# Blocks of 256 rows throughout, expert weights in two transfers, and more low halves on VectorE, in a convolution with eight experts

## The chip, the cores and the metric

One core of one Trainium2 chip. The metric is device time in microseconds (us) of one execution. Three runs of the kernel before gave 1292.79, 1296.68 and 1301.12 us; their median is 1296.68 us.

## What is computed

A softmax-weighted causal convolution over 28672 rows of 192 values is followed by a layer of eight experts, of which each row uses the one with the largest gate product:

```
w   = softmax(weight_gen, over the 7 taps)                 # per row and head
x   = sum over taps k of w[.., k] * x_pad[row + k]         # (28672, 192)
e   = argmax(x @ w_gate)                                   # 8 experts
h   = max(x @ w1[e], 0)                                    # 192 -> 1024
out = prob[e] * (h @ w2[e])                                # 1024 -> 192
```

## The kernel before, in words

The convolution runs in 16 chunks (**stages**) of 14 x 128 = 1792 rows. It is VectorE's main work: lines 358 (products) and 363 (sums), in fp32. Behind a chunk's last sum, line 384 (`halves`) writes the lower fp16 half of its rows, TensorE transposes them (line 398, 42 transposes a chunk) and multiplies them with the gate (line 406, 42 products), VectorE finds the expert and the place of each row (lines 418 to 481, ending in `pos`), and GpSimd scatters the rows, sorted by expert, to a scratch in memory (line 456, 14 scatters a chunk). A table (line 493 on) then says which **blocks** of rows of one expert are complete.

Every number is held as two fp16 halves, so a product is several matmuls. A block's **load** (`load`, from line 549) is four transfers on SyncE's queue: the expert's weights (line 558, 1536.5 KB) and a further 64 partitions of them (line 559, 128 KB), the block's rows `xb`, transposed on the way (line 562), and places and gate factors (line 568). There are three weight buffers, `wt0` to `wt2`. A block then runs in steps of 512 columns of a PSUM bank: with 256 rows four steps, each of 2 x 128 hidden columns; with 512 rows eight steps of 128. In a step the **first products** (lines 594 to 598) fill `p1`, ScalarE takes the upper half of the activated result (`hh`, line 601), and the **low half** `hl` = max(p1, 0) - hh is made in one of two ways: by VectorE in one instruction (line 611), or by TensorE and ScalarE, with a product of `hh` with minus the identity added into `p1` (line 608) and a second activation (line 609). The **second products** (line 627) of `hh` and `hl` follow two to four steps later. `NZ[s]` says how many of the eight slots of a block of stage s go to VectorE; a block of 256 rows uses the first four slots only, so that a 3 there means one of its four. After the last chunk's routing all go to VectorE (`state["done"]`).

The order on each engine is written out ahead of time: `produce()` (the convolution) and `consume()` (the blocks) are two lists of steps with planned times, and the one that is due earlier is written next; TensorE, VectorE, ScalarE and SyncE keep that order. `ahead(n + 1, 2)` in `consume()` issues loads until two blocks beyond the running one are asked for. The last five blocks stand behind conditions; how many of them run depends on the data, here one. All experts' rows together need 115 blocks of 256 rows; the kernel before runs 81 blocks of 256 and 17 of 512.

Of the kernel before, what the change touches and what calls it, by code (L numbers as in the profile page):

```python
# [18 lines left out]
E, F = 8, 1024  # L19
# [6 lines left out]
CAP = N + 256  # L26
TRASH = E * CAP
RW = 400
N256 = 10
SIZES = [(256,)] * N256 + [(512,)] * (len(WID) - N256)  # L30
LAST = 256
PRIO = 2500
# [3 lines left out]
WW = 7 * F + 2  # L36
# [14 lines left out]
LAG2, LAG0, LAGN, LAGL = 2, 4, 1, 4  # L51
HHB, HLB, YB = 6, 6, 12
AV = 4.0
NZ = [0] * 4 + [3] * 12
FINE = 8
DH = 0.65
NSK = 5
# [22 lines left out]
def conv_moe_kernel(ctx: ExitStack, tc: tile.TileContext, x, wgen, wg_in, w1, w2, out):  # L80
    nc = tc.nc
    V, A, GP, PE, SP = nc.vector, nc.scalar, nc.gpsimd, nc.tensor, nc.sync
# [11 lines left out]
    wsc = dram.tile([E, P, WW], F16, name="wsc")  # L94
# [5 lines left out]
    def raw(i):  # L100
        return getattr(i, "ins", i)
# [346 lines left out]
    def no_dep(i, *groups):  # L448
        for g in groups:
            tc.declare_no_dep(i, group=g, reason="rows are disjoint")  # L450
# [87 lines left out]
    nout = [0]  # L538
    loaded = []
    loaded2 = []  # L540
    wts = []
    pools = []

    def written(i, s):

        info = mybir.DependencyInfo(mybir.DependencyClass.Sync, mybir.DependencyReason.DATA)
        for k in scats[s] + (zeros if s == nchunk - 1 else []):
            tc.add_manual_dep(i, k.name, info, reason="rows of the stage")

    def load(s, tb, g, bs):  # L550
        nj = bs // P
        ffn = pools[0]
        with tc.issue_after(loaded[-1]) if loaded else ExitStack():
            rv = SP.value_load(tb[0:1, 0, g:g + 1], min_val=0, max_val=TRASH + 256 - bs)
            ev = SP.value_load(tb[0:1, 1, g:g + 1], min_val=0, max_val=E - 1)
        wt = wts[len(loaded2) % len(wts)]
        loaded2.append(None)
        SP.dma_start(out=wt[:, F:WW], in_=wsc[bass.ds(ev, 1), :, F:WW].rearrange("o p c -> p (o c)"))
        SP.dma_start(out=wt[0:64, 0:F], in_=wsc[bass.ds(ev, 1), 0:64, 0:F].rearrange("o p c -> p (o c)"))
        xb = ffn.tile([P, 3 * 512], F16, name="xb", bufs=3)  # L560
        xv = xb[:, 0:3 * bs].rearrange("p (a b) -> p a b", a=3)
        i = raw(SP.dma_start_transpose(out=xv, in_=scr[bass.ds(rv, bs), 0:384]))
        later = [f"scat{k}" for k in range(s + 1, nchunk)] + ([] if s == nchunk - 1 else ["zero"])
        no_dep(i, *later)
        written(i, s)
        tc.add_to_no_dep_group("loads", i)
        mt = ffn.tile([P, 4, 2], I32, name="mt", bufs=8)
        i = raw(SP.dma_start(out=mt[:, 0:nj, :], in_=scri[bass.ds(rv, bs), 192:194].rearrange("(j p) c -> p j c", p=P)))
        no_dep(i, *later)
        written(i, s)  # L570
        tc.add_to_no_dep_group("loads", i)
        loaded.append(i)
        return wt, xv, mt

    class Block:
        def __init__(self, tiles, bs, via):
# [68 lines left out]
    def step(b=None, f=None):  # L645

        if b is not None:
            b.first(f)
            line.append((b, f))
        n = len(line)  # L650

        def lows(force):
            while at_low[0] < n and (force or n - 1 - at_low[0] >= LAGN):
                g, k = line[at_low[0]]
                g.low(k)
                at_low[0] += 1

        if b is None:
            lows(True)
        more = True  # L660
        while more:
            more = False
            for part, lag in ((1, LAGL), (0, LAG2)):
                i = at_second[part]

                if i < (at_second[0] if part else n) and (b is None or n - 1 - i >= (LAG0 if part == 0 and line[i][1] == 0 else lag)):
                    g, k = line[i]
                    g.second(k, part)
                    at_second[part] += 1
                    more = True  # L670
        if b is not None:
            lows(False)
# [114 lines left out]
    def consume():  # L787
        t = 0.0
        todo = [(s, i, b, bs) for s, stl in enumerate(stages) for i, (bs, g, _) in enumerate(stl) for b in range(g)]
        ready = []  # L790
        skip = todo[len(todo) - NSK:] if NSK else []
        i = raw(SP.dma_start(out=scri[TRASH:TRASH + 256, :].rearrange("(p j) c -> p j c", j=2), in_=zrow.bitcast(I32)))
        no_dep(i, *(f"scat{k}" for k in scats))
        todo = todo[:len(todo) - NSK]

        def ahead(n, k):
            while len(ready) < k and n + len(ready) < len(todo):
                s, i, b, bs = todo[n + len(ready)]
                if s not in avail or (ready and t < avail[s]):
                    break  # L800
                ready.append(load(s, seg_tabs[s][i], b, bs))

        for n, (s, i, b, bs) in enumerate(todo):
            while s not in avail:
                yield None
            if t < avail[s]:
                t = avail[s]
                state["pe"] = 0.0
            yield t
            ahead(n, 1)  # L810
            own = NZ[s] if not state["done"] else NF
            via = [int((k + 1) * own // NF == k * own // NF) for k in range(NF)]
            blk = Block(ready.pop(0), bs, via)
            for k in range(blk.steps):
                with tc.high_priority(offset=PRIO):
                    step(blk, k)
                if k == LAGL - 1:
                    ahead(n + 1, 2)
                if k == blk.steps // 2:
                    blk.gates()  # L820
                t += BLK / NF + NEG * via[k] + state["pe"]
                state["pe"] = 0.0
                yield t
        step()

        def rest(i):
            if i < len(skip):
                loaded.clear()
                with tc.If(cnt > skip[i][2]):
                    for s, j, b, bs in skip[i:i + NSS]:  # L830
                        blk = Block(load(s, seg_tabs[s][j], b, bs), bs, (0,) * NF)
                        for k in range(blk.steps):
                            step(blk, k)
                        blk.gates()
                        step()
                    rest(i + NSS)

        if NSK:
            cnt = nc.values_load(nreal[0][0:1, 0:1], min_val=0, max_val=64)
            rest(0)  # L840
        yield 1e9

    ET = mybir.EngineType
    with tc.manual_schedule(engines={ET.DVE, ET.Activation, ET.PE, ET.SP}):
        pg, cg = produce(), consume()
        tp, tcon = 0.0, None
        with tc.tile_pool(name="stg", bufs=WB) as pool:
            stg.append(pool)
            while not state["prep"]:
                tp = next(pg)  # L850
        pools.append(ctx.enter_context(tc.tile_pool(name="ffn", bufs=2)))
        for i in range(3):
            wts.append(pools[0].tile([P, WW], F16, name=f"wt{i}", bufs=1))
            A.activation(out=wts[i][64:P, 0:F], in_=ones[64:P, 0:1].to_broadcast([64, F]), func=AF.Copy, scale=0.0)
        while tp < 1e9 or tcon is None or tcon < 1e9:
            if tp < 1e9 and (tcon is None or tp + state["own"] <= tcon):
                tp = next(pg)
                if tcon is None:
                    tcon = next(cg)
            else:  # L860
                tcon = next(cg)
# [26 lines left out]
```

## Time and profile before

| | us |
|---|---|
| median of 3 runs | 1296.68 |
| the profiled execution | 1297.31 |
| its span, from first to last instruction | 1295.6 |

In the rows further down, times count from the span's start. A busy TensorE (PE) is not a TensorE at its peak, since the durations of its matmuls overlap; how far apart their starts lie tells its pace. PEld is its weight load. "Idle before" is the time an engine did nothing ahead of an instruction, and the name behind the arrow is what ended it.

### The profile page before, as it was taken

Reading aid. Unit: us, or ns where it says so; the run is one execution under the profiler, and the core shown is the slowest. Engines: PE = TensorE matmul, PEld = TensorE weight load, DVE = VectorE, ACT = ScalarE, POOL = GpSimd, SP = SyncE. Lnnn points to the kernel's source line nnn. Section 1 sums busy time; section 2 is a strip of 40 time slices with the busy share of each in tenths; the row PEclk is TensorE's granted clock in tenths of the full one; section 3 lists DMA queues with packets and bytes.
Section 4 is the critical chain, followed back from the end, with each engine's and each line's share of the span. In section 5 each row is a group of like instructions: output and inputs, shape, how many; then the busy total and the mean of one; then the engine's idle time right before and its main releaser. Section 6 shows DMA issues by size and latency. Waiting matters only on the chain.

```text
span 1295.6 us, 29303 instructions
## 1 busy us (share of the span) xinstructions
PE 1155.5 (89%) x11223; PEld 955.5 (74%) x11223; DVE 998.1 (77%) x1285; ACT 766.1 (59%) x1401; POOL 778.2 (60%) x611
## 2 busy tenths in 40 slices
PE   1485499899999999989998998999999999999997
PEld 0143277788888888888987887776777777789886
DVE  8998999899998999999999999999443333323322
ACT  5888665667775676666766666665743333333332
POOL 3236616558888888988878898888762222222222
PEclk9787799999999999999999999999999999999999
DMA  9747777788879899998889889855777665498883
GB/s 323 229 159 254 240 239 225 233 249 264 269 216 279 221 287 252 275 286 231 281 263 273 245 262 294 231 156 139 192 227 158 145 148 148 138 254 217 239 244 94
DMA packets 190754, 293.94 MB, mean 227 GB/s; under 512 B 135695, under 2 KB 155264, under 8 KB 176017
## 3 DMA queue, kind: packets, MB, share of 16 engines
q1 hardware_dynamic: 168816, 247.02, 66.3%
q0 software_dynamic: 21792, 44.99, 12.2%
q8 instruction: 90, 1.47, 0.5%
q14 instruction: 56, 0.45, 0.1%
HBM read 208.89 MB, written 61.03 MB: 208 GB/s over the span
## 4 chain that ended last, share of the span: by engine, by line
PE 41%; DMA 15%; DVE 15%; POOL 9%; issue 5%; ACT 2%; SPq 1%; POOLq 0%; DVEq 0%; ACTq 0%
PE po L627 18%; DMA xb<-scr 9%; POOL scr L456 7%; DVE tmp L358 5%; DVE acc L363 5%; PE p L594 4%; DMA scr<-rows,pos 4%; PE p L598 4%; PE p L596 4%; PE p L597 4%; PE p L595 4%; DMA out_dram<-y,mt 2%; POOL out_dram L635 2%; PE p L608 2%; DVE rows L384 1%
## 5 line engine op out<-in xcount | busy, mean ns | idle before, releaser
L635 POOL DMA_INDIRECT out_dram<-y,mt x230 | 307.3, 1336 | 340.8 <-ACT y L634 281.7
L601 ACT ACTIVATE hh<-p 128x512 f16<-128x512 f32 x460 | 276.0, 600 | 316.9 <-PE p L598 312.0
L456 POOL DMA_INDIRECT scr<-rows,pos x224 | 387.2, 1729 | 113.8 <-issue 60.4
L627 PE MATMUL po<-wt,hh 128*128 128x192 f16 x3680 | 367.1, 248 | 0.7 <-ACT y L634 0.7
L611 DVE SCALAR_TENSOR_TENSOR hl<-p,hh 128x512 f16<-128x512 f32 x215 | 148.1, 689 | 248.5 <-ACT hh L601 248.5
L627 PEld LDWEIGHTS <-hh 128*128 128x128 f16 x3680 | 314.0, 99 | 7.6 <-issue 0.8
L358 DVE TENSOR_TENSOR tmp<-xin,wgt 128x1344 f32<-128x1344 f32 (+1 forms) x168 | 289.6, 1750 | 1.3
L363 DVE TENSOR_TENSOR acc<-acc,tmp 128x1344 f32<-128x1344 f32 (+1 forms) x168 | 289.4, 1750 | 1.0
L594 PE MATMUL p<-xb,wt 128*128 128x256 f16 (+1 forms) x784 | 228.8, 292 | 51.3 <-DMA xb<-scr 42.8
L609 ACT ACTIVATE hl<-p 128x512 f16<-128x512 f32 x245 | 146.6, 598 | 147.5 <-PE p L608 142.7
L596 PE MATMUL p<-xb,wt 128*128 128x256 f16 (+1 forms) x784 | 229.2, 292 | 0.0
L598 PE MATMUL p<-xb,wt 128*128 128x256 f16 (+1 forms) x784 | 229.2, 292 | 0.0
L597 PE MATMUL p<-xb,wt 128*128 128x256 f16 (+1 forms) x784 | 229.2, 292 | 0.0
L595 PE MATMUL p<-xb,wt 128*128 128x256 f16 (+1 forms) x784 | 229.0, 292 | 0.0
L627 PE MATMUL po<-wt,hl 128*128 128x192 f16 x1840 | 228.1, 247 | 0.0
L627 PEld LDWEIGHTS <-hl 128*128 128x128 f16 x1840 | 165.1, 98 | 33.3
L594 PEld LDWEIGHTS <-wt 128*128 128x128 f16 x784 | 76.7, 98 | 63.9 <-issue 58.1
L595 PEld LDWEIGHTS <-wt 128*128 128x128 f16 x784 | 76.7, 98 | 29.2 <-issue 6.6
L608 PE MATMUL p<-hh,negi 128*128 128x512 f16 x245 | 92.8, 379 | 5.4 <-ACT hh L601 5.4
L598 PEld LDWEIGHTS <-wt 128*128 128x128 f16 x784 | 77.0, 98 | 23.9
L597 PEld LDWEIGHTS <-wt 128*128 128x128 f16 x784 | 77.0, 98 | 23.9
L596 PEld LDWEIGHTS <-wt 128*128 128x128 f16 x784 | 76.9, 98 | 23.9
(123 smaller groups left out, 1100.6 us busy)
## 6 DMA issues: line engine op xcount, KB each, us to landing
wt<-wsc SPq DMA_DIRECT2D x98, 1536.5 KB
xin<-in_x_dram SPq DMA_DIRECT2D x15, 1344.0 KB
wt<-wsc SPq DMA_DIRECT2D x98, 128.0 KB
wgt<-in_weight_gen_dram SPq DMA_DIRECT2D x16, 392.0 KB
wsc<-wt SPq DMA_DIRECT2D x8, 768.5 KB
wa<-in_moe_w_dram SPq DMA_DIRECT2D x8, 768.0 KB
wa<-in_moe_w_dram SPq DMA_DIRECT2D x8, 512.0 KB
wsc<-wt SPq DMA_DIRECT2D x16, 256.0 KB
```

The lines of the kernel that those rows point to most:

```text
L358: V.tensor_tensor(out=t[:, a:b, :].rearrange("p t (h g) -> p (t h) g", g=G), in0=xv, in1=wv, op=ALU.mult)
L363: V.tensor_tensor(out=acc[:, a:b, :], in0=acc[:, a:b, :], in1=t[:, a:b, :], op=ALU.add)
L456: i = raw(GP.indirect_dma_start(scri, bass.IndirectOffsetOnAxis(ap=pos[:, t:t + 1], axis=0), rows_t[s % 3].bitcast(I32)[:, t, 0:RW // 2], ...
L594: PE.matmul(o, lhsT=wt[:, F + fs:F + fs + P], rhs=xv[:, 0, :], start=i == 0, stop=False)
L595: PE.matmul(o, lhsT=wt[:, F + fs:F + fs + P], rhs=xv[:, 1, :], start=False, stop=False)
L596: PE.matmul(o, lhsT=wt[:, 3 * F + fs:3 * F + fs + P], rhs=xv[:, 0, :], start=False, stop=False)
L597: PE.matmul(o, lhsT=wt[:, 2 * F + fs:2 * F + fs + P], rhs=xv[:, 2, :], start=False, stop=False)
L598: PE.matmul(o, lhsT=wt[:, fs:fs + P], rhs=xv[:, 2, :], start=False, stop=i == self.each - 1)
L601: A.activation(out=hh, in_=p1, func=AF.Relu, scale=1.0 - 2.0 ** -11 if self.via[k] else 1.0)
L611: V.scalar_tensor_tensor(out=hl, in0=p1, scalar=0.0, in1=hh, op0=ALU.max, op1=ALU.subtract)
L627: PE.matmul(o, lhsT=h[:, js], rhs=w2, start=(f == 0 and j % 2 == 0 and not part and w == 0), stop=part == 1 and f == NF - 1 and (j % 2 == ...
L635: i = raw(GP.indirect_dma_start(out, bass.IndirectOffsetOnAxis(ap=self.mt[:, j, 1:2], axis=0), y, None, bounds_check=N - 1, oob_is_err=False))
```

## The change

Three things are changed. All 16 stages cut their rows into blocks of 256 (`N256`). The big weight transfer is cut in two: the part for the first products goes out with the 128 KB, x and the places, as before two blocks ahead but already behind a block's first step; the part for the second products goes out by a function of its own, `seconds()`, behind the fourth step, or ahead of the next load. And `NZ` now gives VectorE no low halves up to stage 4 (the stages count from 0), two of a block's four in stage 5 (slots 2 and 4), and all from stage 6.

```
-N256 = 10
+N256 = 16
-NZ = [0] * 4 + [3] * 12
+NZ = [0] * 5 + [5] * 1 + [8] * 10
...
     def load(s, tb, g, bs):
...
+        seconds()
-        SP.dma_start(out=wt[:, F:WW], in_=wsc[bass.ds(ev, 1), :, F:WW].rearrange("o p c -> p (o c)"))
+        SP.dma_start(out=wt[:, F:4 * F], in_=wsc[bass.ds(ev, 1), :, F:4 * F].rearrange("o p c -> p (o c)"))
         SP.dma_start(out=wt[0:64, 0:F], in_=wsc[bass.ds(ev, 1), 0:64, 0:F].rearrange("o p c -> p (o c)"))
...
+        halfway.append((wt, ev))
         return wt, xv, mt
+
+    def seconds():
+        while halfway:
+            wt, ev = halfway.pop(0)
+            SP.dma_start(out=wt[:, 4 * F:WW], in_=wsc[bass.ds(ev, 1), :, 4 * F:WW].rearrange("o p c -> p (o c)"))
...
-            ahead(n, 1)
+            if not ready:
+                ahead(n, 1)
+                seconds()
...
             for k in range(blk.steps):
                 with tc.high_priority(offset=PRIO):
                     step(blk, k)
+                if k == 0:
+                    ahead(n + 1, 2)
                 if k == LAGL - 1:
-                    ahead(n + 1, 2)
+                    seconds()
```

In the conditional blocks at the end `seconds()` follows the load at once. There are now 115 blocks of 256 rows and none of 512.

On VectorE, where chunk 13 of the convolution begins its preparation (`mx`, `wgt` and `sm` belong to the softmax, `tmp` and `acc` to the convolution, `hl` is a low half), the row before reads:

```order
L363 TENSOR_TENSOR acc<-acc,tmp 128x1344 x2
L305 TENSOR_REDUCE mx<-wgt 128x112
L307 TENSOR_TENSOR wgt<-wgt,mx 128x784
L358 TENSOR_TENSOR tmp<-xin,wgt 128x1344 x2
L611 SCALAR_TENSOR_TENSOR hl<-p_10932,hh 128x512
L363 TENSOR_TENSOR acc<-acc,tmp 128x1344 x2
L358 TENSOR_TENSOR tmp<-xin,wgt 128x1344 x2
L336 TENSOR_REDUCE sm<-wgt 128x112
```

and now, at the same place:

```order
L363 TENSOR_TENSOR acc<-acc,tmp 128x1344 x2
L305 TENSOR_REDUCE mx<-wgt 128x112
L619 SCALAR_TENSOR_TENSOR hl<-p_12012,hh 128x512
L307 TENSOR_TENSOR wgt<-wgt,mx 128x784
L619 SCALAR_TENSOR_TENSOR hl<-p_12056,hh 128x512
L358 TENSOR_TENSOR tmp<-xin,wgt 128x1344
L619 SCALAR_TENSOR_TENSOR hl<-p_12126,hh 128x512
L358 TENSOR_TENSOR tmp<-xin,wgt 128x1344
L619 SCALAR_TENSOR_TENSOR hl<-p_12155,hh 128x512
L363 TENSOR_TENSOR acc<-acc,tmp 128x1344 x2
L619 SCALAR_TENSOR_TENSOR hl<-p_12187,hh 128x512
L358 TENSOR_TENSOR tmp<-xin,wgt 128x1344
```

Line 619 is the old line 611. A low half now stands behind nearly every instruction of the convolution. Counted over the whole order, 55 low halves stood ahead of the last chunk's line 384 on VectorE, and 229 stand there now; ahead of that chunk's first transpose TensorE had 73.0 blocks' worth (in blocks of 256 rows) of first products, and has 89.75 now. Of the products of line 608, 126 are left of 245.

On SyncE's queue, one load in the middle of the program (in brackets, what the queue waits for there: a DMAHW name is an earlier transfer of the queue, a DMASW name one of GpSimd's; ISA and TENSOR_LOAD rows read the table) before:

```order
L558 DMA wt1_1136<-wsc_79 128x6146 [waits DMAHW7_49,PE_49,Activation_49]
L559 ISA
L559 DMA wt1_1136<-wsc_79 64x1024 [waits DMAHW0_49]
L562 ISA
L562 DMA_TRANSPOSE xb_9721<-scr_78 128x3x256 [waits DMAHW1_49]
L568 ISA
L568 DMA mt_9723<-scr_78 128x2x2 [waits DMAHW2_49,DMASW3_49,DMASW2_49]
```

and now, from the second part of one block's weights to the x of the next:

```order
L581 DMA wt2_1138<-wsc_79 128x3074 [waits DMAHW4_49,PE_49,Activation_49]
L555 TENSOR_LOAD tb7_8724
L555 ISA x2
L556 TENSOR_LOAD tb7_8724
L556 ISA x2
L560 ISA
L560 DMA wt0_1134<-wsc_79 128x3072 [waits DMAHW5_49]
L561 ISA
L561 DMA wt0_1134<-wsc_79 64x1024 [waits DMAHW6_49]
L564 ISA
L564 DMA_TRANSPOSE xb_10888<-scr_78 128x3x256 [waits DMAHW7_49]
```

The wait for TensorE has moved from the front of a load to the second part of the weights of the load ahead of it, so that the next block's first part and its x go out behind the same wait that used to release one whole load, one block earlier relative to the block that uses them.

## Rows read from the trace of the kernel before

**Rows 1.** The profile page: the span; for each engine its busy time, its share of the span and its instructions; the packets and bytes of the DMAs; and of its part on DMA issues (count, KB each) that of the big weight transfer.

```profile
span 1295.6 us, 29303 instructions
...
PE 1155.5 (89%) x11223; PEld 955.5 (74%) x11223; DVE 998.1 (77%) x1285; ACT 766.1 (59%) x1401; POOL 778.2 (60%) x611
...
DMA packets 190754, 293.94 MB, mean 227 GB/s; under 512 B 135695, under 2 KB 155264, under 8 KB 176017
...
wt<-wsc SPq DMA_DIRECT2D x98, 1536.5 KB
```

**Rows 2.** The busy time of each engine (number of instructions) in stretches of the span; the last three columns are the granted TensorE clock, the mean busy share of the 16 DMA engines, and what they moved in GB/s.

```profile
core 0: us, PE busy (x) PEld busy (x) DVE busy (x) ACT busy (x) POOL busy (x), PEclk, DMA share, GB/s
247.00:469.00 222.00, 211.09 (x2291) 189.69 (x2289) 210.03 (x241) 154.62 (x287) 174.29 (x108) 0.99 0.84 249
469.00:858.00 389.00, 370.59 (x3989) 328.59 (x3988) 380.99 (x499) 260.05 (x481) 330.56 (x224) 1.00 0.89 257
...
920.00:1120.00 200.00, 200.00 (x1694) 143.23 (x1692) 68.68 (x135) 83.34 (x173) 71.37 (x73) 1.00 0.65 167
```

**Rows 3.** VectorE's instructions in order of time, merged (start us, us, instruction), in the middle of the stretch in which it is full.

```profile
704.44 3.02 DVE L358 TENSOR_TENSOR tmp<-xin,wgt 128x1344 f32<-128x1344 f32 x2
707.38 0.68 DVE L611 SCALAR_TENSOR_TENSOR hl<-p,hh 128x512 f16<-128x512 f32 x1
707.98 3.01 DVE L363 TENSOR_TENSOR acc<-acc,tmp 128x1344 f32<-128x1344 f32 x2
```

**Rows 4.** All instructions of line 611 (the low halves on VectorE) between 247 and 858 us: duration least/median/most in ns, first and last start, shape; and the idle time of VectorE ahead of them, by what ended it (us, times).

```profile
L611 DVE SCALAR_TENSOR_TENSOR hl<-p,hh x46: 669/682/692, 398.9 to 853.7; 128x512 f16<-128x512 f32 x46
...
  ACT hh L601: 4.9, 3
```

**Rows 5.** Who waited for whom in the whole span: us in total, times, longest us.

```profile
DVE hl L611 <- ACT hh L601: 248.5, 163, 7.7
...
PE p L594 <- DMA xb<-scr: 42.8, 22, 16.8
```

**Rows 6.** The stretch from the start of one block of 256 rows to the start of the 15th after it, which is the last block ahead of the conditional ones (columns as in the second group).

```profile
1131.73:1266.53 134.80, 126.79 (x1322) 117.56 (x1321) 42.20 (x61) 49.56 (x110) 31.55 (x33) 1.00 0.84 233
```

**Rows 7.** The waits of SyncE's queue, from which all loads are issued: us in total, times, longest us.

```profile
SPq L558 <- PE po L627: 521.7, 91, 14.3
```

**Rows 8.** SyncE's queue in the stretch of group 6: weights and x of one load, and the weights of the next.

```profile
1203.30 0.34 SPq L558 DMA_DIRECT2D wt<-wsc  x1
...
1204.83 1.55 SPq L562 DMA_TRANSPOSE xb<-scr  x1
...
1211.71 0.34 SPq L558 DMA_DIRECT2D wt<-wsc  x1
```

**Rows 9.** Of the chain that ended last (start us, us, what), a transfer of x and the last output.

```profile
1239.63 8.58 DMA xb<-scr
...
1275.91 12.96 DMA out_dram<-y,mt
```

**Rows 10.** Groups of instructions by line, engine, operation and shape: busy us, mean ns of one, idle time before them and what ended it.

```profile
L456 POOL DMA_INDIRECT scr<-rows,pos x224 | 387.2, 1729 | 113.8 <-issue 60.4 <-ACT si L244 26.2 <-DVE qi L494 14.2
...
L611 DVE SCALAR_TENSOR_TENSOR hl<-p,hh 128x512 f16<-128x512 f32 x215 | 148.1, 689 | 248.5 <-ACT hh L601 248.5
...
L496 DVE CAST av<-qi 1x8 f32<-1x8 int32 x15 | 3.2, 212 | 0.5
```

**Rows 11.** TensorE at the first transposes of the last chunk of the convolution.

```profile
920.47 0.61 PE L398 MATMUL p<-idh,rows 128*128 128x128 f16 x8
...
922.99 1.06 PE L398 MATMUL p<-idh,rows 128*128 128x128 f16 x16
923.88 0.38 PE L594 MATMUL p<-xb,wt 128*128 128x512 f16 x1
```

**Rows 12.** TensorE in order of time at the gate products of line 406 and at a product of line 608, each with the matmul that follows it.

```profile
610.84 0.65 PE L406 MATMUL route<-wg,xt 128*128 128x16 f16 x20
611.35 0.27 PE L594 MATMUL p<-xb,wt 128*128 128x256 f16 x1
...
613.43 0.38 PE L608 MATMUL p<-hh,negi 128*128 128x512 f16 x1
613.64 0.27 PE L594 MATMUL p<-xb,wt 128*128 128x256 f16 x1
```

**Rows 13.** TensorE in a block of 512 rows, one step (128 of 1024 hidden columns): its first matmul, its first second product, and the first matmul of the next step.

```profile
1002.64 0.38 PE L594 MATMUL p<-xb,wt 128*128 128x512 f16 x1
...
1003.72 0.49 PE L627 MATMUL po<-wt,hl 128*128 128x192 f16 x4
...
1004.71 0.38 PE L594 MATMUL p<-xb,wt 128*128 128x512 f16 x1
```

**Rows 14.** The same in a block of 256 rows, one step (256 of 1024 hidden columns).

```profile
1206.50 0.27 PE L594 MATMUL p<-xb,wt 128*128 128x256 f16 x1
...
1207.59 0.49 PE L627 MATMUL po<-wt,hl 128*128 128x192 f16 x4
...
1208.58 0.27 PE L594 MATMUL p<-xb,wt 128*128 128x256 f16 x1
```

**Rows 15.** Two short stretches in which the DMA engines were full (columns as in the second group).

```profile
455.00:475.00 20.00, 18.81 (x195) 16.93 (x193) 19.43 (x21) 13.86 (x24) 18.02 (x13) 1.00 1.05 320
494.00:506.00 12.00, 9.98 (x104) 9.05 (x103) 11.76 (x17) 7.62 (x17) 9.94 (x10) 1.00 1.03 265
```

More of the change, by code (lines that the diff above doesn't have):

```diff
@@ L540, in conv_moe_kernel @@
     loaded2 = []
+    halfway = []
     wts = []
@@ L831, in rest @@
                         blk = Block(load(s, seg_tabs[s][j], b, bs), bs, (0,) * NF)
+                        seconds()
                         for k in range(blk.steps):
```

## The prediction

> **What bounds the kernel now.** I began with the page's busy shares: TensorE 89%, VectorE 77% [rows 1]. They are averages over two stretches, so I went on to the stretches themselves [rows 2]. From 469 to 858 us VectorE works 381.0 of 389 us (98%) and TensorE 370.6 (95%). From 920 us on, with the convolution over, TensorE works 200.0 of 200 us and VectorE a third. So VectorE sets the pace up to some 920 us, with TensorE close behind, and TensorE sets it from there.
>
> VectorE's order in time shows that it really is without a gap there, and what a low half costs it [rows 3]: one starts at 707.38, the next instruction at 707.98. That is 0.60 us, less than the duration of 0.68, since neighbours overlap. Whether a low half waits for TensorE is read from line 611 alone: of 46 between 247 and 858 us only three waited, 4.9 us together [rows 4]. So nearly all of the 248.5 us for which VectorE waited for `hh` [rows 5] lies behind the convolution and costs nothing.
>
> Behind it, the run of 256-row blocks takes 134.8 us for 15 blocks, 8.99 us each [rows 6], while TensorE's own work in a block is 8.32 us (below). The rest is waiting for x, 42.8 us in the whole span [rows 5]. Its cause is in SyncE's queue: the weights of a load wait for TensorE to free a weight buffer, 521.7 us in all [rows 7]. A load goes out at 1203.30, its x at 1204.83, the next load at 1211.71 [rows 8], and an x in flight there takes 8.58 us [rows 9]. x is issued one block before it is used and takes about a block.
>
> **The change, part by part.**
>
> *Low halves on VectorE.* By the two orders, 55 stood ahead of the last chunk's line 384 and 229 stand there now: 174 more. At 0.60 us [rows 3] this is 104.4 us; at the mean duration of 0.69 us [rows 10] it would be 120. I take 0.60, the start-to-start time in just this situation, and keep the other end. A sixteenth table is new (stage 10 had no complete block of 512): 14 small instructions, each near the 0.21 us of line 496 [rows 10], 3 us.
>
> *What VectorE idles in addition.* It idled 8.0 us of 389 (2%) [rows 2]; the same share of 107 added us is 2 us. But balance is now closer. VectorE's work without low halves is 998.1 - 148.1 = 850 us [rows 1, 10], 53.1 us a chunk. In the middle of the new order 8.25 blocks, 33 low halves, fall to a chunk: 53.1 + 33 x 0.60 = 72.9 us. TensorE has 8.25 x 8.32 us, 42 transposes and 42 gate products to do, 72.0 us (prices below). Two full engines with four handovers a block: if the idle share doubled over the eight chunks from 469 us, it would be 2% of 580, 12 us. I take 8, between 2 and 12. In it is the entry into stage 14: by the order its first block starts 3.75 blocks (31 us) after its places are known, while 14 scatters at 1.73 us [rows 10] and an x of 8.58 us need 33.
>
> *First transposes of the last chunk.* They start at 920.5 us [rows 11]. New: 920.5 + 104.4 + 3 + 8 = 1035.9 us.
>
> *TensorE's prices.* The product of line 608 takes 0.21 us (613.43 to 613.64) [rows 12], and 119 of them go, 25 us. While VectorE sets the pace, what they give back is not time but room, and it is what makes 8.25 blocks a chunk fit. Twenty gate products take 0.51 us [rows 12]. A step of a 512-row block takes 2.07 us, eight of them 16.56; a step of a 256-row block takes 2.08 us, four of them 8.32 [rows 13, 14]. So the 17 blocks that fall in two cost 17 x 0.08 = 1.4 us in all. Sixteen transposes take 0.89 us [rows 11]; with the gate products this is 3.4 us a chunk.
>
> The start-to-start time of the first products is 0.216 us with 512 columns and 0.109 with 256 [rows 13, 14]: half the columns, half the time. The Trainium skill (TensorE: Matmul & The Clock Gate, section Back-to-back issue gap) gives sustained 131 ns for 512 columns and 81 for 128, by which halving would be dear: an estimate of 98 ns for 256, put on the 680 matmuls of 512 columns, would add 680 x (196 - 131) ns = 44 us. The same section's gap for a matmul by itself, 216 ns, is what the trace of this kernel shows in a full stream; I add nothing.
>
> *The load in two parts.* There are 115 x 5 transfers instead of 98 x 4, 183 more at 0.34 us of issuing [rows 8], 62 us of a queue that spends 521.7 us waiting [rows 7]: hidden. By the new order x of a block follows a wait that ends as the second block before it starts, instead of the one before it. Then 1.5 + 8.6 us have 16.6 us to pass in. I take 8.4 us a block behind the convolution, 0.08 above TensorE's own time; the ends are 8.32 (nothing waits) and 8.99 (as now) [rows 6].
>
> *Bytes.* 17 more loads of 1.7 MB make 323 MB of 294 [rows 1]. A block moves 233 GB/s x 8.99 us = 2.09 MB [rows 6]. A chunk moves now about 257 GB/s x 55.6 us (a seventh of the 389 us) = 14.3 MB [rows 2], 5.6 blocks in it 11.7, so the convolution 2.6. New: 8.25 x 2.09 + 2.6 = 19.8 MB in 74 us, 268 GB/s, where 257 went at a share of 0.89: about 0.93. Behind it 2.09 MB in 8.4 us, 249 GB/s. Stretches of 320 GB/s occur [rows 15], so this hides; the third rival is what happens if not.
>
> *Behind the last transposes.* 114 blocks stand ahead of the conditional ones, and 89.75 have had their first products. To the start of the last of the 114 it is 113 - 89.75 = 23.25 blocks x 8.4 = 195.3 us, and 3.4 us for the last chunk's transposes and gate products. From there to the end it was 1295.6 - 1266.5 = 29.1 us [rows 1, 6], with an output of 12.96 us as its last piece [rows 9]; nothing there changes.
>
> **Sum.** 1035.9 + 3.4 + 195.3 + 29.1 = 1263.7 us of span, and 1.7 us around it (1297.3 - 1295.6): 1265 us, against 1297.3 of the same execution; the median of the runs shown is 0.6 us below that. The convolution ends 115 us later, and 25.25 blocks are left instead of 42: 147.4 us less. Net 32 us, 2.5%.
>
> **The rivals.**
>
> First, *the two full engines wait for each other*. For it: 72.9 against 72.0 us a chunk leaves no room, and every low half now ties one to the other. Against it: 43 of 46 low halves found their input ready [rows 4]. If each of the 61.5 blocks from chunk 7's to chunk 15's transposes lost what a block loses now behind the convolution, 8.99 - 8.32 = 0.67 us, this would be 41 us instead of 8: 1298 us. Something under it, 1285 to 1305, is no change within 1%, about what a measurement of this kernel can tell.
>
> Second, *VectorE idles no more than now and nothing waits*: 2 instead of 8 us, and 8.32 us a block: 1257 us; with low halves filling gaps that VectorE has now, a few us less, to 1246.
>
> Third, the other side: *the 16 DMA engines become the bound* from 469 us on. Five transfers a block, none over 770 KB, might run at a lower rate. If they carried only the 233 GB/s seen in the last stretch [rows 6], a chunk would take 19.8 MB / 233 = 85 us instead of 74, 11 us times 7.5 chunks, and a block 8.99 us: 1362 us. At 249 GB/s it is 79.5 us a chunk, 1306. It is slower than now below some 253 GB/s and by over 1% below 248; I let 1330 stand for it. Against it: 265 and 320 GB/s at a full queue [rows 15], with the same x and outputs in them. The Trainium skill speaks for it (DMA: Bandwidth & Descriptors, sections Anatomy of one DMA and Bandwidth): transfers should be at least 1 MiB, and each of those that GpSimd issues has a fixed cost of about 2.0 us. An estimate by that cost, if transfers did not overlap, is 8.25 x 2.0 = 16.5 us more a chunk. That the engines showed a mean share of 1.05 over 20 us [rows 15] says that transfers do overlap here.
>
> Fourth, *x comes as late as now*, because the second part of the weights stands ahead of the next x in the queue and waits longer than I think: 8.99 us a block behind the convolution, 23.25 x 0.59 = 14 us more, 1279 us.
>
> **How the numbers follow.** Forecast, 1252 to 1283: 0.58. Engines waiting for each other: 0.20. No waits, under 1252: 0.08. DMA engines the bound: 0.08. x as late as now: 0.06, which lies within the forecast's side. Faster by over 1% (under 1284): 0.58 + 0.08 + 0.06 = 0.72; within 1%: 0.20; slower: 0.08. The range goes from 1246, the second rival's low end, to 1297, into the first; what it leaves out is the DMA bound and the upper part of the first rival.
>
> **What would show it.** Right: 126 products of line 608 and 334 low halves on VectorE, 0.60 us apart from the next instruction; VectorE at 97% or more up to the last chunk; its first transposes at 1026 to 1046 us; 8.3 to 8.5 us a block behind them; waits for x there of a few us in all. Wrong: VectorE waiting for `hh` well before the convolution ends (first rival); DMA share at 1 with under 255 GB/s (third); x issued only one block ahead (fourth); first transposes past 1055 us, which would also say that 0.60 us was too little.

## The result, and the profile after

The changed kernel takes 1258.91 us, the median of 4 runs (1256.48 to 1260.33), against 1296.97 of the kernel before on the same chip (4 runs, 1292.79 to 1301.12). The ratio is 0.9705, 95% interval 0.967 to 0.974: 38 us faster. A second run of both kernels, beside the experiments, gave 1256.03 against 1296.46, ratio 0.9703 (0.9679 to 0.9728). The forecast was 1265 (1246 to 1297). The chip is seen in a faster and a slower state: a ratio compares executions in the faster one alone, while a median is that of all.

The page's first lines and, from its part on DMA issues, the two parts of the weights (count, KB each), which answer to [rows 1]:

```profile
span 1256.6 us, 31171 instructions
...
PE 1131.6 (90%) x11784; PEld 1014.4 (81%) x11784; DVE 1062.3 (85%) x1421; ACT 708.1 (56%) x1299; POOL 793.4 (63%) x611
...
DMA packets 211946, 323.03 MB, mean 257 GB/s; under 512 B 138894, under 2 KB 158463, under 8 KB 209744
...
wt<-wsc SPq DMA_DIRECT2D x115, 768.5 KB
wt<-wsc SPq DMA_DIRECT2D x115, 768.0 KB
```

TensorE's share of the span hardly moved (89 to 90%), VectorE's went from 77 to 85%, since 64 us more of its work fit into a span that is 39 us shorter. Where they fit is seen by stretches, as in [rows 2] and [rows 6] (busy time of each engine, number of instructions; then granted clock, DMA share, GB/s):

```profile
core 0: us, PE busy (x) PEld busy (x) DVE busy (x) ACT busy (x) POOL busy (x), PEclk, DMA share, GB/s
602.00:891.00 289.00, 285.29 (x3204) 269.71 (x3201) 284.80 (x404) 151.32 (x287) 218.21 (x155) 1.00 1.03 284
...
1144.29:1219.23 74.94, 74.94 (x795) 70.86 (x794) 24.89 (x36) 28.73 (x64) 17.50 (x18) 1.00 0.99 248
```

The first stretch is four chunks in the middle. VectorE and TensorE both work 99% of it, beside DMA engines at a share of 1.03 that move 284 GB/s. The second is nine blocks behind the convolution: 74.94 / 9 = 8.33 us a block, and TensorE idles in none of it (8.99 us before).

VectorE in order of time in that first stretch, as in [rows 3], and all low halves between 470 and 1025 us (number, duration least/median/most, first and last start) with the idle time ahead of them, as in [rows 4]:

```profile
616.41 0.68 DVE L619 SCALAR_TENSOR_TENSOR hl<-p,hh 128x512 f16<-128x512 f32 x1
617.02 3.02 DVE L358 TENSOR_TENSOR tmp<-xin,wgt 128x1344 f32<-128x1344 f32 x2
...
L619 DVE SCALAR_TENSOR_TENSOR hl<-p,hh x228: 627/673/693, 475.2 to 1024.9; 128x512 f16<-128x512 f32 x114
...
  ACT hh L609: 15.2, 10
```

A low half still takes 0.61 us from its start to the next, and of 228 only 10 found their input not ready, 15.2 us together. The last chunk's first transposes, as in [rows 11], and the busy time up to them before and after:

```profile
1030.09 0.61 PE L398 MATMUL p<-idh,rows 128*128 128x128 f16 x8
```
```profile
0.00:920.47 920.47, 796.66 (x7879) 665.36 (x7880) 877.86 (x1076) 622.44 (x1097) 667.22 (x498) 0.96 0.83 245
```
```profile
0.00:1030.09 1030.09, 914.30 (x9436) 808.98 (x9437) 982.71 (x1268) 620.17 (x1111) 721.79 (x538) 0.96 0.92 261
```

Up to there VectorE works 982.71 - 877.86 = 104.9 us more and idles 47.4 instead of 42.6 us; TensorE works 117.6 us more and idles 115.8 instead of 123.8. So the convolution ends 109.6 us later, and TensorE has spent that time on blocks: 25.25 are left instead of 42.

Last, the waits (us in total, times, longest us), as in [rows 5] and [rows 7], and SyncE's queue at one load, as in [rows 8]:

```profile
PE p L602 <- DMA xb<-scr: 32.4, 12, 14.4
...
SPq L581 <- PE po L635: 269.0, 85, 10.4
SPq L564 <- DMA scr<-rows,pos: 70.9, 14, 12.7
SPq L570 <- DMA out_dram<-y,mt: 54.7, 26, 12.4
```
```profile
1202.86 0.33 SPq L581 DMA_DIRECT2D wt<-wsc  x1
1204.60 0.34 SPq L560 DMA_DIRECT2D wt<-wsc  x1
...
1205.77 1.35 SPq L564 DMA_TRANSPOSE xb<-scr  x1
...
1211.19 0.33 SPq L581 DMA_DIRECT2D wt<-wsc  x1
```

The x that goes out at 1205.77 is that of the block that starts at 1219.23, 13.5 us later. Of the 32.4 us of waiting for x, 14.4 are the first block's.

### The profile page after: what moved, and what is told of

It reads as the page before. It is cut to its first block, busy times and chain, and to the rows that moved or that the text cites. A ratio compares the mean times of both kernels' runs of the same rounds, so it can differ in the third digit from the quotient of the medians.

```text
span 1256.6 us, 31171 instructions
## 1 busy us (share of the span) xinstructions
PE 1131.6 (90%) x11784; PEld 1014.4 (81%) x11784; DVE 1062.3 (85%) x1421; ACT 708.1 (56%) x1299; POOL 793.4 (63%) x611
## 4 chain that ended last, share of the span: by engine, by line
DVE 47%; PE 29%; DMA 9%; issue 7%; SPq 3%; ACT 3%; POOL 2%; POOLq 0%; DVEq 0%; ACTq 0%
DVE tmp L358 14%; DVE acc L363 14%; PE po L635 13%; DVE hl L619 5%; PE p L602 3%; PE p L606 3%; PE p L603 3%; PE p L605 3%; PE p L604 3%; DMA out_dram<-y,mt 3%; DVE acc L358 3%; DVE rows L384 3%; DMA xb<-scr 2%; DMA scr<-rows,pos 1%; DMA wt<-wsc 1%
## 5 line engine op out<-in xcount | busy, mean ns | idle before, releaser
L643 POOL DMA_INDIRECT out_dram<-y,mt x230 | 351.0, 1526 | 275.4 <-ACT y L642 215.9
L456 POOL DMA_INDIRECT scr<-rows,pos x224 | 360.9, 1611 | 121.5 <-issue 61.2
L619 DVE SCALAR_TENSOR_TENSOR hl<-p,hh 128x512 f16<-128x512 f32 x334 | 225.1, 680 | 148.7 <-ACT hh L609 148.4
L602 PE MATMUL p<-xb,wt 128*128 128x256 f16 x920 | 251.9, 274 | 39.3 <-DMA xb<-scr 32.4
L606 PE MATMUL p<-xb,wt 128*128 128x256 f16 x920 | 252.2, 274 | 0.0
L605 PE MATMUL p<-xb,wt 128*128 128x256 f16 x920 | 252.2, 274 | 0.0
L603 PE MATMUL p<-xb,wt 128*128 128x256 f16 x920 | 252.0, 274 | 0.0
L604 PE MATMUL p<-xb,wt 128*128 128x256 f16 x920 | 252.0, 274 | 0.0
L602 PEld LDWEIGHTS <-wt 128*128 128x128 f16 x920 | 90.3, 98 | 42.4 <-issue 24.2
L603 PEld LDWEIGHTS <-wt 128*128 128x128 f16 x920 | 90.2, 98 | 29.6 <-issue 14.6
L399 ACT ACTIVATE xt<-p 128x1024 f16<-128x1024 f16 x96 | 86.5, 925 | 37.7 <-PE p L398 37.7
L617 ACT ACTIVATE hl<-p 128x512 f16<-128x512 f32 x126 | 75.7, 601 | 53.9 <-PE p L616 53.8
L604 PEld LDWEIGHTS <-wt 128*128 128x128 f16 x920 | 90.4, 98 | 11.0
L606 PEld LDWEIGHTS <-wt 128*128 128x128 f16 x920 | 90.4, 98 | 11.0
L605 PEld LDWEIGHTS <-wt 128*128 128x128 f16 x920 | 90.4, 98 | 11.0
```

What stands on the lines that cost most here:

```text
L456: i = raw(GP.indirect_dma_start(scri, bass.IndirectOffsetOnAxis(ap=pos[:, t:t + 1], axis=0), rows_t[s % 3].bitcast(I32)[:, t, 0:RW // 2], ...
L602: PE.matmul(o, lhsT=wt[:, F + fs:F + fs + P], rhs=xv[:, 0, :], start=i == 0, stop=False)
L603: PE.matmul(o, lhsT=wt[:, F + fs:F + fs + P], rhs=xv[:, 1, :], start=False, stop=False)
L604: PE.matmul(o, lhsT=wt[:, 3 * F + fs:3 * F + fs + P], rhs=xv[:, 0, :], start=False, stop=False)
L605: PE.matmul(o, lhsT=wt[:, 2 * F + fs:2 * F + fs + P], rhs=xv[:, 2, :], start=False, stop=False)
L606: PE.matmul(o, lhsT=wt[:, fs:fs + P], rhs=xv[:, 2, :], start=False, stop=i == self.each - 1)
```

## The experiments

Theory A is the prediction's: up to the last chunk VectorE sets the pace; TensorE follows as long as blocks and their x are there in time; behind it TensorE alone counts. Its rivals are named in each expectation. Each kernel is compared with the kernel before on the same chip. The chips differ: the kernel before took 1296 to 1299 us on some, 1361 and 1380 on two others, so a ratio is compared with one from another chip only with care.

**The three parts, one by one and in pairs.** One part alone:

```
e1_split:   before + the load in two parts
e2_n256:    before, N256 = 16
e3_nz:      before, NZ = [0] * 5 + [5] * 1 + [8] * 10
```

> The kernel before with the load in two parts alone (sizes and NZ as before). Theory A (VectorE paces up to the last chunk, TensorE behind it): nothing is won while VectorE paces; behind it the 18 blocks of 256 rows at the end run at 8.33 instead of 8.99 us, -12 us: 1285 us. Rival B (TensorE paces throughout, so every wait for x counts): the waits for x behind the first block, 42.8 - 16.8 = 26 us, go too: 1271 us.

> The kernel before with blocks of 256 rows in all stages alone (whole loads, NZ as before). Both theories: TensorE's own work is the same within 1.4 us, but the 24 block units that ran as 512-row blocks behind the last transposes now wait for x like the others, 8.99 instead of 8.28 us each: +17 us, 1314 us. If blocks of 256 rows were better in themselves: under 1297 us.

> The kernel before with the new NZ alone (512-row blocks from stage 10, whole loads). Theory A: some 104 us more low halves on VectorE ahead of the last transposes, as many blocks fewer behind them, and 25 us less on TensorE; the 256-row blocks keep their waits for x (about 12 us behind the convolution, and some in stages 6 to 9, where both engines are full): 1275 us. Rival C (the gain comes from the loads): no better than 1290 us.

On the chip where before takes 1360.65: the load in two parts alone 1324.55, ratio 0.9732 (0.9681 to 0.9783); 256 rows alone 1390.41, 1.0229 (1.0157 to 1.03); the low halves alone 1411.83, 1.0345 (1.0274 to 1.0417). The first two have the expected sign and are larger than expected. The first gains 36 us, where A gave 12 and rival B, by which TensorE sets the pace throughout, 26: this is nearer to B, and e5 below is what decides between the two. What it gains on a chip where before takes 1297 us was not run. The third fell on the wrong side for A: more low halves on VectorE, with the blocks and the load as before, lose 3%. Rival C (the gain comes from the loads) leaves that open.

Two parts, the third as before:

```
e6_oldnz:   after, NZ = [0] * 4 + [3] * 12
e7_mixed:   after, N256 = 10
e4_nosplit, e11_nosplit:  before, N256 = 16, NZ = [0] * 5 + [5] * 1 + [8] * 10
```

> The changed kernel with the NZ of before (256 rows and the load in two parts stay). Theory A: the last chunk's first transposes come at some 920 us as before with 73 blocks behind them, and the 40 blocks to the last unconditional one take 8.35 us each: 1288 us where the kernel before takes 1297, 29 us over the changed kernel. Rival C (the gain comes from the loads): within 8 us of the changed kernel.

> The changed kernel with 512-row blocks from stage 10 on (the load in two parts and the new NZ stay). If the size of the blocks changes nothing but the number of loads: within 5 us of the changed kernel. Theory A, with what the run of the new NZ alone showed (TensorE out of blocks at the first stage of 512 rows, 12.7 us for the next chunk's rows and 25.1 us for x): TensorE runs dry there, some 35 us over the changed kernel.

> The changed kernel with the load in one piece as before (256 rows and the new NZ stay). Theory A: the 25 blocks behind the last transposes run at 8.99 instead of 8.33 us, +17 us; in the stretch ahead of it a block has 8.8 us while a load issued one block ahead needs about 10, so TensorE waits there as well, 0.5 us or more a block, +30 us: about 1305 us. Rival C (the two parts matter behind the convolution only): 1276 us. Rival D (the two parts are worth nothing): 1259 us.

> The changed kernel with the load in one transfer per block, weights behind x as before; all blocks of 256 rows and the new sharing of low halves stay. Theory A (VectorE sets the pace to the last chunk, and a load that comes late for its block takes blocks out of TensorE's store, which the first 512-row stages then want): on a chip where the kernel before takes 1297, about 1305 (ratio 1.006), with waits of TensorE for x of over 60 us in sum where the changed kernel has 32, and a gap of TensorE of over 10 us in the segment of the first 512-row stage. Rival: the loss that two runs of this kernel showed belongs to the chips on which they ran (there the kernel before took 1361 and 1380); on one where the kernel before takes 1297 the whole load costs nothing: within 6 us of the changed kernel, ratio 0.970 to 0.975, TensorE's waits for x as in it. On a chip where the kernel before takes over 1340 the two are not told apart.

| two parts | 256 rows | low halves | ratio (interval) | kernel before on that chip |
|---|---|---|---|---|
| yes | yes | | 0.9988 (0.9961 to 1.0015) | 1296 |
| yes | | yes | 1.0144 (1.0113 to 1.0175) | 1296 |
| | yes | yes | 1.0461 (1.037 to 1.0552) | 1361 |
| | yes | yes | 1.0253 (1.022 to 1.0285) | 1299 |
| yes | yes | yes | 0.9703 (0.9679 to 0.9728) | 1296 |

The third row is e4, the fourth e11. No pair is faster than before; all three together are, by 3%. Each pair shows what the missing part is there for.

*Without the new low halves* (e6, 1295.7 us; A expected 1288, the rival a time within 8 of the changed kernel, which falls): VectorE is done with the convolution early, TensorE is not relieved. The busy time up to the last chunk's transposes, in this kernel:

```profile
0.00:923.49 923.49, 797.15 (x8054) 684.20 (x8055) 877.93 (x1087) 622.99 (x1104) 688.88 (x501) 0.96 0.88 252
```

In span and in the busy time of TensorE, VectorE and ScalarE this is the row of the kernel before to within some 3 us, and 42.25 blocks are left behind it, against 42. Why it ends 8 us later than A gave is open.

*Without 256 rows in the later stages* (e7, 1315.78 us; expected some 35 us over the changed kernel, measured 60): the last chunk's transposes stand at VectorE's pace as in the changed kernel, but 32.25 blocks are left. The stretch with the first block of 512 rows, and that block's first matmul (in brackets the idle time before it):

```profile
1026.12 0.61 PE L398 MATMUL p<-idh,rows 128*128 128x128 f16 x8
```
```profile
789.00:885.00 96.00, 56.06 (x495) 41.23 (x496) 83.17 (x120) 29.82 (x52) 59.73 (x36) 0.77 0.43 125
```
```profile
833.45 0.58 PE L602 MATMUL p<-xb,wt 128*128 128x512 f16 x1 [25.26 <-DMA xb<-scr]
```

In this one chunk TensorE works 56 of 96 us. From 784 us on it has no further block whose x is there, so VectorE works on the convolution from 791.96 to 821.40 without a low half, and the third of GpSimd's 14 scatters of the rows that the next block needs is held there (start, us):

```profile
791.94 18.67 POOL L456 DMA_INDIRECT scr<-rows,pos  x1 [0.30 <-issue]
```
```profile
829.45 1.47 SPq L564 DMA_TRANSPOSE xb<-scr  x1
```

The last of the 14 scatters ends at 827.9, x goes out at 829.45, and TensorE waits 25.3 us for it in one piece; VectorE idles too (it works 83 of 96). The granted clock is 0.77 in the mean here: behind the idle stretch TensorE is at its lower level of 1.2 GHz, and its first products of 512 columns start 0.43 us apart (833.83, 834.26) instead of 0.21 (838.79, 839.00). So the 256 rows do not save matmul time; they are complete earlier and keep TensorE supplied.

*Without the load in two parts* (e11, 1331.45 us against 1299.02). A expected 1305 and waits for x of over 60 us; the rival said that the loss of e4 belongs to its chip and would vanish here. It did not vanish, so the rival falls, and with it those of e4, by which the two parts are worth something behind the convolution only, or nothing; the loss is larger than A gave. A stretch of the middle chunks, TensorE's waits for x in all, VectorE's for `hh` from chunk 7's transposes to the last chunk's (471 to 1076 us) and the same of the changed kernel (457 to 1030 us), and x of one block behind the convolution:

```profile
615.00:858.00 243.00, 223.46 (x2431) 209.04 (x2429) 215.50 (x304) 115.02 (x217) 131.61 (x109) 0.97 0.88 249
```
```profile
PE p L594 <- DMA xb<-scr: 85.2, 52, 17.7
```
```profile
DVE hl L611 <- ACT hh L601: 52.5, 35, 5.5
```
```profile
DVE hl L619 <- ACT hh L609: 16.5, 11, 3.4
```
```profile
1189.54 9.09 DMA xb<-scr
```
```profile
1198.76 0.27 PE L594 MATMUL p<-xb,wt 128*128 128x256 f16 x1 [1.85 <-DMA xb<-scr]
```

x goes out 9.2 us ahead of its block, takes 9.1, and TensorE waits. In the middle VectorE then works 89% instead of 99%, because its low halves wait for TensorE (and it for x), and DMA moves 249 instead of 284 GB/s. The gap of over 10 us at 512 rows that the expectation named has no place in this kernel, which has no such block; TensorE's idle time is spread, 3 to 9 us a chunk. Against the changed kernel 13 us are lost up to chunk 7's transposes (470.7 instead of 457.4 us), where VectorE has no low halves yet, 32 from there to the last chunk's (605 instead of 573 us), and 25 behind them (251 instead of 227). Of these 25, A's price covers 17: the last 15 blocks ahead of the conditional one start between 1161.98 and 1297.91 us, 9.06 us each, close to the 8.99 of the kernel before [rows 6]. The 8.25 blocks right behind the transposes take 10.1 us each, with the longest wait for x there (4.6 us, ending at 1141.80); why they are slower is open.

With the load in two parts its first part and x also go out at another point, behind a block's first step instead of its fourth. No run has one without the other, so what is shown is the worth of both together.

A third run of this kernel, beside e8 and e9 below, on the chip where before takes 1380:

> The changed kernel with the load in one piece, the kernel of the fourth run, on a chip on which the kernel before takes its usual 1297 us. Theory A: as there, 17 us behind the last chunk and some 30 ahead of it over the changed kernel: about 1305 us, no faster than the kernel before. Rival (that run was slow because of its chip alone): 1259 to 1276 us.

It took 1420 to 1458 us and says no more than e4: on that chip the expectation's two theories are not told apart by time.

**Which engine sets the pace up to the last chunk.** Line 606, one of the five first products, is left out in the blocks of stages 6 and up, which takes eight matmuls of 0.109 us off TensorE in a block and nothing off VectorE:

```
+    blk = Block(ready.pop(0), bs, via, s > 5)        # lean
-    PE.matmul(o, lhsT=wt[:, fs:fs + P], rhs=xv[:, 2, :], ...)
+    if not self.lean:
+        PE.matmul(o, lhsT=wt[:, fs:fs + P], rhs=xv[:, 2, :], ...)
```

> The changed kernel itself, as the yardstick on the chip on which the next three run (the four before ran where the kernel before took 1361 us instead of 1297). Theory A (its loads are early enough not to be waited for): the ratio to the kernel before stays near 0.97, or gets better where the kernel before waits longer. Rival: the ratio is nearer 1 where transfers are slower.

> The changed kernel without the last of the five first products (line 606: the low half of the last 64 inputs times the weights' rest) in all unconditional blocks from stage 6 on: 79 blocks x 8 x 0.109 us = 69 us less work on TensorE. Theory A (VectorE paces up to the last chunk's transposes): nothing there, 23 to 24 blocks x 0.87 us = 21 us behind them: 21 us under the changed kernel. Rival B (TensorE paces throughout): 69 us under it.

It takes 1239.78 us, 16 less than the changed kernel beside it; A expected 21 less, the rival (TensorE sets the pace throughout) 69. The last chunk's transposes, the middle chunks, and TensorE's waits for low halves (lines 603 and 621 are the changed kernel's 602 and 619):

```profile
1024.74 0.61 PE L398 MATMUL p<-idh,rows 128*128 128x128 f16 x8
```
```profile
596.00:887.00 291.00, 264.45 (x2951) 246.55 (x2949) 287.02 (x406) 149.81 (x288) 212.89 (x156) 0.99 1.04 283
```
```profile
PE p L603 <- DVE hl L621: 28.6, 27, 3.5
```

The transposes stand at 1025, where the changed kernel has 1024 in the run beside it. A TensorE with a tenth less to do in a block turns this into idle time (264 of 291 us) and waits for VectorE's low halves; only behind the convolution is it faster (214 instead of 227 us). Of the 20 us that A gave there 13 came, since TensorE waits for x there 1.7 and 4.7 us, ending at 1038 and 1090, where the changed kernel beside it has one wait of 1.6. That VectorE sets the pace in the middle chunks, and not TensorE, is shown. The DMA engines are full there too, at a share of 1.04, which this run can't change; but VectorE idles only 4 of the 291 us, so faster transfers could give back no more than that.

**Two variants of the changed kernel,** on the chip where before takes 1380.03:

```
e8_s4:   NZ = [0] * 4 + [3] + [5] + [8] * 10
e9_mt16: mt = ffn.tile(..., bufs=16)          # 8 before
```

> The changed kernel with one of four low halves on VectorE already in stage 4. Theory G (an indirect DMA of GpSimd gets on only where VectorE runs an instruction that does not read two tensors of SBUF, such as a low half; at 445.8 us, where none stood for 17.6 us, the outputs fell behind, SyncE's queue waited 54.7 us for them in all, and x came late five times between 475 and 548 us): the long GpSimd instruction at 446 us falls under 8 us and most of the 11.8 us of waits for x there go; 7 more low halves cost VectorE 4 us ahead of the last chunk. Net 1252 us where the changed kernel takes 1256. Rival (those waits cost nothing, VectorE paces): 4 us slower.

> The changed kernel with 16 instead of 8 buffers for places and gate factors (mt). Theory G: the late outputs then hold no mt buffer that a load needs, SyncE's queue waits for them no more (54.7 us now), x is in time between 475 and 548 us, and the 11 us for which VectorE idles in that stretch shrink to some 4: 6 to 7 us faster than the changed kernel. Rival: the late GpSimd is not what makes x late there: no difference beyond 2 us.

e8 took 1351.37, ratio 0.9813 (0.9765 to 0.9861). e9 took 1376.69 in the median of six; its ratio of 0.9818 (0.9747 to 0.989) is formed of two of them, 1350.42 and 1359.49. Both beat the kernel before by some 2%; the changed kernel itself was not run on that chip, so whether either beats it is not settled. The waits that theory G named did go. In e8 no indirect DMA takes over 4.2 us between 360 and 620 us, and TensorE waits for x three times in all, 8.4 us. In e9 SyncE's queue waits 2.7 us for late outputs at line 570 instead of 54.7, and TensorE waits for x twice, 17.2 us, 14.8 of them in one piece.

## Why the prediction was right

*VectorE sets the pace to the last chunk, at 0.60 us a low half.* Shown by e5 for the middle chunks. VectorE works 98.5% of them; over the whole way from 457 us to the last chunk it is 95.5%, under the 97% that was named as a sign of being right. 174 low halves and a sixteenth table were put at 107.4 us; VectorE's busy time grew by 104.9. The duration of 0.69 us would have given 120.

*VectorE's added idle time.* Put at 8 us, between 2 and 12; 4.8 were measured. With the term above, the transposes came at 1030.1 instead of 1035.9 us. But the 4.8 us are a sum of two that nearly cancel, and that they do is luck. Before and after, up to chunk 7's transposes, and then from there on in the changed kernel:

```profile
0.00:469.00 469.00, 366.56 (x3362) 294.40 (x3363) 439.33 (x503) 324.88 (x551) 283.94 (x243) 0.92 0.81 247
```
```profile
0.00:457.00 457.00, 361.74 (x3327) 289.98 (x3328) 435.20 (x497) 325.36 (x554) 287.33 (x228) 0.93 0.84 249
457.00:1030.09 573.09, 552.56 (x6112) 519.00 (x6110) 547.51 (x772) 294.81 (x557) 434.46 (x311) 0.99 0.98 270
```

Up to chunk 7 VectorE idles 21.8 instead of 29.7 us, and the transposes come some 12 us earlier; the other 4 are low halves of stage 4 that have moved behind them. The prediction, which starts from the last chunk's 920.5 us, has nothing of this. The gain belongs to the load in two parts: e6, which has it beside the old `NZ`, is there at 457.5 us, e11, with whole loads, at 470.7. From there on VectorE idles 25.6 instead of 12.9 us: 12.6 more, over the top of the range. They do not lie where the prediction put them either: 11.1 us stand between 457 and 602 us, where x comes late, 10.3 from 891 us on, and only 4.2 in the four full chunks between. e6 shows the same pair without the new low halves: some 11 us ahead of the kernel before at chunk 7, 3 us behind it at the last chunk. The closer balance, for which the 8 us were put, costs nothing to be seen there, and the first rival (two full engines that wait for each other) did not come about: 10 waits of 228 low halves.

*TensorE behind the convolution.* 25.25 blocks left, as counted. Predicted 8.4 us a block, measured 8.33, which is TensorE's own time. From the start of the last block ahead of the conditional one (1227.55) to the end it is 29.05 us, predicted 29.1. So the whole difference of 7 us in the span, 1263.7 to 1256.6, is made of 5.8 us before the transposes and some 1.3 behind them.

*TensorE's room.* 72.0 us against VectorE's 72.9 were worked out for a chunk of 8.25 blocks; chunks 9 to 12 took 72 to 73, with about 1 us of VectorE's idle time in each. The 512-column start-to-start time of 0.216 us was rightly taken from the trace: halving the columns cost TensorE nothing visible.

*Bytes.* 323 MB as predicted, and 284 GB/s at a share of 1.03 in the full stretch, where 268 at 0.93 was expected: the engines were nearer to their bound than I thought, and the third rival's price of 233 GB/s was that of a stretch in which they were not full (a share of 0.84 [rows 6]). The Trainium skill (DMA: Bandwidth & Descriptors, section Bandwidth) asks for transfers of 1 MiB and more; in this case the load cut into parts of 768 KB wins: a ratio to the kernel before of 0.9705 with it, 1.0253 with whole loads of 1536.5 KB (e11). x goes out 13.5 us ahead of its block instead of 9.2; transfers of another size at the same point of the queue were not run. The third rival's estimate of 16.5 us more a chunk, worked out from a price for transfers that GpSimd issues while these are SyncE's, did not come about: the full chunks take 72 to 73 us.

*What the prediction had too small.* The fourth rival, x as late as before, was priced at 14 us, all behind the convolution. e11 has x that late (9.06 us a block behind the convolution), and it costs 70 us of span, 45 of them ahead of the last chunk's transposes. The step that failed is that a late x was counted as idle TensorE only where TensorE sets the pace. Where both engines are full, TensorE's wait becomes VectorE's: its waits for `hh` grow from 16.5 to 52.5 us in a stretch that gets 32 us longer. The 13 us up to chunk 7 are the same omission seen from the other side: an earlier x was given no worth there. By the same omission the prediction gave the 256 rows nothing but a cost of 1.4 us, and e7's expectation was 25 us short.

## What to carry to other kernels

An engine that sets the pace in one stretch and idles in the next can take work from the one that is full in both, but only if that one is kept supplied for the longer stretch: here the shift of low halves gained 38 us with smaller blocks and earlier x, and lost 19 to 32 us without one of them. The prices of the parts did not add up here; a part should be tried beside the others, not alone. Take the price of an instruction on a full engine from start to start, and price a late input by what both engines lose. Where a forecast starts from a late point of the old trace, look also at what the change does ahead of that point.

## What the runs showed of the hardware

An indirect DMA on GpSimd can be held over many VectorE instructions. In the changed kernel, GpSimd and VectorE (start, us) at the same time:

```profile
444.50 0.99 POOL L643 DMA_INDIRECT out_dram<-y,mt  x1 [0.30 <-issue]
445.80 17.58 POOL L643 DMA_INDIRECT out_dram<-y,mt  x1 [0.30 <-issue]
463.68 0.97 POOL L643 DMA_INDIRECT out_dram<-y,mt  x1 [0.30 <-issue]
```
```profile
444.71 3.01 DVE L358 TENSOR_TENSOR acc<-xin,wgt 128x1344 f32<-128x1344 f32 x2
...
459.51 3.01 DVE L363 TENSOR_TENSOR acc<-acc,tmp 128x1344 f32<-128x1344 f32 x2
462.45 0.95 DVE L305 TENSOR_REDUCE mx<-wgt 128x112 f32<-128x784 f32 x1
463.33 0.67 DVE L619 SCALAR_TENSOR_TENSOR hl<-p,hh 128x512 f16<-128x512 f32 x1
```

The same instruction takes 0.97 to 0.99 us on either side and 17.58 in between, and it ends at 463.38, behind a reduction and at the start of a low half, the first instructions on VectorE for 17 us that do not read two operands in SBUF. In e7 the 18.67 us begin with such a stretch (791.96) and end with the reduction that closes it (809.71 to 810.66). The Trainium skill (SBUF — State Buffer, section SBUF: two separate sides) says that a VectorE instruction with two SBUF inputs and a GpSimd instruction that reads SBUF exclude each other: whichever starts first holds the port pair that they share for its whole instruction. Most rows agree with that: in e7 the scatters behind 812 us take 1.16 us and follow each other every 1.47 us, which is the pace of VectorE's products there. The long holds do not agree; they last for ten such instructions and more, and what decides between the two is open.

The sharing of low halves changes how often it happens. The scatters of line 456 in the kernel before, 469 to 858 us, and in the changed one from 601 us on (duration least/median/most in ns):

```profile
L456 POOL DMA_INDIRECT scr<-rows,pos x98: 960/1168/11690, 468.4 to 841.7; - x98
```
```profile
L456 POOL DMA_INDIRECT scr<-rows,pos x91: 954/1759/3767, 601.1 to 1029.9; - x91
```

The longest hold falls from 11.7 to 3.8 us while the median rises. Before 600 us, where VectorE has no or few low halves, the changed kernel still has the 17.58 us, and late outputs there hold up SyncE's queue (43.7 of the 54.7 us in the waits above). e8 and e9, on one chip, test this: e9 has no low half in stage 4, like the changed kernel, e8 one of four (the long instruction in e9, and the outputs of e8 between 360 and 620 us):

```profile
451.99 17.61 POOL L643 DMA_INDIRECT out_dram<-y,mt  x1 [0.30 <-issue]
```
```profile
L643 POOL DMA_INDIRECT out_dram<-y,mt x52: 967/1115/3907, 382.5 to 619.4; - x52
```

So with one of four low halves in that stage this hold does not arise. That a low half or a reduction ends one is read from the order in time alone. Nor did a run test what makes two of the chips slower: the whole-load kernel has a span of 1414.4 us on one of them (e4, mean granted clock 0.930) and 1327.0 on a usual one (e11, 0.958), with the same instructions.
